# A planner that lays out one core's instructions: which tasks GpSimd may take, and when a tile may be taken early

## The chip, the core and the metric

The kernel runs on one core of one Trainium2 chip. The metric is the device time of one execution in microseconds (us). The core's engines work side by side: TensorE (PE in the profile; PEld is its weight load), VectorE (DVE), ScalarE (ACT), GpSimd (POOL) and SyncE (SP, which issues the transfers). Each engine runs its own instructions strictly in the order in which the program lists them, and waits where an operand is not there yet.

## The reference

Three layers follow each other, all in float32 (the weights come as float64 bit patterns, and are rounded on the chip):

```python
# 1. retention, B=2, H=8 heads, S=768, D=64
state = gamma * state + k[t] v[t]^T;  y[t] = scale * q[t] @ state
x = y.transpose(0, 2, 1, 3).reshape(1536, 512)
# 2. softplus layer, d_ff = 2048
h = x @ w_in;  x = (maximum(h, 0) + log1p(exp(-abs(h)))) @ w_out
# 3. gated layer, d_ff = 1536
xn = x / sqrt(mean(x * x, -1) + 1e-6) * rms_g
g = xn @ w_gate
out = (g / (1 + exp(-g)) * (xn @ w_val)) @ w_out2
```

## The kernel before

**Tiling.** The 1536 tokens are three blocks of 512 columns. A projection is a set of matmuls of 128x512. Every operand is split into a high and a low part (`hi` is a rounding copy, `lo` the rest), and each product is three matmuls. Blocks 0 and 1 go through a seven-product scheme (the class `Seven`, a Strassen form), which needs sums of activations (T1 to T4, and B11, B21, B22) and of weights (`s`, split into `ws_s`). The third block, "lone", is multiplied plainly. Its four output banks stay occupied in PSUM all through layer 2, so of eight banks four are left to turn over.

**Stages.** Until about 72 us the retention layer runs, written by hand in `batch`, `turn`, `scores` and so on. Everything after that is put into a `Plan` as tasks: layer 2 to about 302 us, then a passage in which the mean square of each block is taken (`mean`: TensorE sums squares, VectorE runs twelve tiny instructions on 128x4, called `small` and `root_t`), spread over the columns by TensorE and ScalarE (`along`, the tile `root`), multiplied in (`scaled`, L1185), and made into the B and T parts; then from about 361 us six passes over the gated layer (pass 0 begins within the passage).

**Weights.** A 128x512 weight takes eight tasks: ScalarE reads its low and high words (tiles `c` and `a`), VectorE shifts and joins bits (`w`, L880 and L883), GpSimd adds the integers (`c`, L886, called the total here), VectorE multiplies (`a`, L888), ScalarE rounds to `hi`, and VectorE or GpSimd subtracts for `lo`. 63 weights go through the plan.

**What sets the order.** The planner runs while the program is built. It gives every task a due time (`late`), followed back from TensorE's list, and then, step by step, starts the task that can start first by its own costs, on the engine that can take it. Tasks made with `("V", "G")` can go to VectorE or GpSimd (`less`, `rounded`, `part_lo`, the weight sums); GpSimd takes one only if its due time is at least `spare` us after its start. TensorE may take any of the next six products. What comes out is a fixed list of instructions for each engine; on the chip nothing is chosen any more. A task that opens a tile takes it from a pool (`R4`: two-wide tiles, `R2`: one-wide tiles, `PB`: PSUM banks, `ST`: landing tiles of the weight transfers). In `R4` and `R2` it is held back while fewer tiles are free than tasks with an earlier due time will want:

```python
ahead = 0 if p.loose else sum(1 for w in p.wanted if w < t.late - 1e-9)
if len(p.free) < n + ahead:
    return None
```

Helpers record many operations, so one line stands for many: L932 is every matmul of the plan, L828 every two-operand operation on SBUF tiles (`two_in`), L832 every copy of ScalarE.

Of the kernel before, what the change touches and what calls it, by code (L numbers as in the profile page):

```python
# [23 lines left out]
PAIRS = 2  # L24
WINDOW = 6
SLACK = 5.0
SPARE = 3.0
TINY = 1.125 * 2.0 ** -15


# [6 lines left out]
class Buf:  # L37

    def __init__(self, pool, name, dt=F32, tile=None, tag=None, at=0.0):
        self.pool, self.name, self.dt, self.tile, self.tag, self.last = pool, name, dt, tile, tag, at  # L40
        self.left, self.marks, self.opener = 0, {}, None


class Pool:

    def __init__(self, make, tags, at=0.0):
        self.make, self.free, self.wanted = make, [(at, tag) for tag in tags], []


class Task:  # L50
# [6 lines left out]

class Plan:

    def __init__(self, window=6, slack=3.0, spare=3.0):  # L60
        self.tasks, self.window, self.slack, self.spare = [], window, slack, spare

    def add(self, engs, took, do, reads=(), writes=(), opens=(), soft=False, rest=None):
        t = Task(engs, took, do, soft, rest or (took[0] if type(took) is tuple else took))
# [36 lines left out]
    def run(self, free):  # L101
        tasks = self.tasks
        at = 0.0
        for t in tasks:
            if t.engs == "P":
                t.nominal = at
                at += t.took
        for t in reversed(tasks):
            late = t.nominal if t.engs == "P" else at
            for h, off in t.heirs:  # L110
                late = min(late, h.late + off - t.rest - 0.05)
            if t.engs != "P":
                for b in t.bufs:
                    if b.pool and b.pool.psum:
                        ends = [w.nominal + w.took for w, _ in t.needs if w.engs == "P"]
                        if ends:
                            late = min(late, max(ends) + self.slack)
            t.late = late
        for t in tasks:
            for b in t.opens:  # L120
                b.pool.wanted.append(t.late)
            t.open_needs = len({id(o) for o, _ in t.needs})
            t.ready = 0.0
        for p in {id(b.pool): b.pool for t in tasks for b in t.opens}.values():
            p.wanted.sort()
        line = [t for t in tasks if t.engs == "P"]
        able = {e: [] for e in "AVGS"}
        for t in tasks:
            if not t.open_needs and t.engs != "P":
                for e in t.engs:  # L130
                    able[e].append(t)
        busy = {"V": 0.0, "G": 0.0}
        done = 0

        def start(t, e):
            st = max(free[e], max([o.end + LAT.get(o.eng + e, 0.06) - off for o, off in t.needs], default=0.0))
            want = {}
            for b in t.opens:
                want.setdefault(id(b.pool), [b.pool, 0])[1] += 1
            for p, n in want.values():  # L140
                ahead = 0 if p.loose else sum(1 for w in p.wanted if w < t.late - 1e-9)
                if len(p.free) < n + ahead:
                    return None
                st = max(st, sorted(p.free)[n - 1][0])
            if e == "V" and t.soft:
                st = max(st, busy["G"])
            if e == "G":
                st = max(st, busy["V"], busy["G"] + 0.02)
                if t.engs != "G" and t.late < st + self.spare:
                    return None  # L150
            return st

        while done < len(tasks):
            best = None
            for e in "PAVGS":
                if e == "P":
                    some = [t for t in line[:self.window] if all(o.end is not None for o, _ in t.needs)]
                else:
                    some = able[e]
                cands = [(start(t, e), n, t) for n, t in enumerate(some)]  # L160
                cands = [c for c in cands if c[0] is not None]
                if not cands:
                    continue
                first = min(c[0] for c in cands)
                near = [c for c in cands if c[0] <= first + 0.05]
                if e == "P":
                    pick = min(near, key=lambda c: c[2].nominal)
                    if pick[2] is not line[0] and any(len(b.pool.free) < 3 for b in pick[2].opens):
                        lead = [c for c in cands if c[2] is line[0] or not c[2].opens]
                        if lead:  # L170
                            first = min(c[0] for c in lead)
                            pick = min([c for c in lead if c[0] <= first + 0.05], key=lambda c: c[2].nominal)
                else:
                    pick = min(near, key=lambda c: (c[2].late, c[1]))
                if best is None or pick[0] < best[0] - 1e-9:
                    best = pick[0], e, pick[2]
            st, e, t = best
            for b in t.opens:
                p = b.pool
                p.free.sort()  # L180
                n = next(i for i, f in enumerate(p.free))
                _, b.tag = p.free.pop(n)
                p.wanted.remove(t.late)
                b.tile = p.make(b.tag, b)
            t.do(e)
            t.eng, t.start = e, st
            took = t.took[t.engs.index(e)] if type(t.took) is tuple else t.took
            t.end = st + (t.rest if e == "P" else took)
            free[e] = st + took - FILL.get(e, 0.0)
            if e == "S":  # L190
                free[e] = st + 0.06
                t.end = self.land(st, took)
            if e == "G":
                busy["G"] = t.end
            if e == "V" and t.soft:
                busy["V"] = t.end
            if e == "P":
                line.remove(t)
            else:
                for x in t.engs:  # L200
                    able[x].remove(t)
            for b in t.bufs:
                b.left -= 1
                b.last = max(b.last, t.end)
                if not b.left and b.pool:
                    b.pool.free.append((b.last + 0.06, b.tag))
            seen = set()
            for h, _ in t.heirs:
                if id(h) in seen:
                    continue  # L210
                seen.add(id(h))
                h.open_needs -= 1
                if not h.open_needs and h.engs != "P":
                    for x in h.engs:
                        able[x].append(h)
            done += 1
# [9 lines left out]
def retention_softplus_swiglu(ctx: ExitStack, tc: tile.TileContext, q, k, v, w_in, w_out,  # L226
# [28 lines left out]
    def row(tag, name, dt=F32):  # L255
        return mem.tile([P, N], dt, tag=tag, name=name)
# [207 lines left out]
    x, tr, tp = {}, {}, {}  # L464
# [337 lines left out]
    def two_wide(tag, b):  # L802
# [4 lines left out]
    R2 = Pool(lambda tag, b: row(tag, b.name, b.dt), [f"s2_{n}" for n in range(10)] + ["c0", "c1", "a0", "a1", "a2", "w", "s0", "s1"]  # L807
              + ["t0", "t1", "t2", "st", "fd", "r", "ms"], 3.0)
    PB = Pool(lambda tag, b: ps.tile([P, N], F32, tag=tag, name=b.name), [])
    PB.free = [(0.6 * n, f"ps{i}") for n, i in enumerate(oldest)]  # L810
    ST = Pool(lambda tag, b: mem.tile([P, N, 2], U32, tag=tag, name=b.name), st_free, 0.0)
    for p in (R4, R2, PB, ST):
        p.psum, p.loose = p is PB, p is PB or p is ST
    plan = Plan(WINDOW, SLACK, SPARE)
    add = plan.add
    A_PS, A_SB, V_2, G_2 = 0.6, 0.63, 0.69, 1.3

    def mine(pool, name, tile, tag, at=1.0):
        return Buf(pool, name, None, tile, tag, at)
# [103 lines left out]
    G = {key: mine(R4, "g", g_t[key], g_at[key]) for key in g_t}  # L923
# [36 lines left out]
    def psum(name):  # L960
        return Buf(PB, name)
# [89 lines left out]
    class Seven:  # L1051

        def __init__(self, nm, p):
            self.nm, self.p = nm, p
            self.Q, self.R, self.W = psum("Q"), psum("R"), psum("W")
# [326 lines left out]
    p = NPR - 1  # L1382
# [47 lines left out]
```

## Time and profile before

| | |
|---|---|
| median of 3 runs | 611.44 us (609.17 to 611.69) |
| the profiled execution's own time | 611.97 us |
| its span on the core | 610.1 us |
| PE busy | 593.9 us, 97% |
| DVE busy | 504.5 us, 83% |
| ACT busy | 359.3 us, 59% |
| POOL busy | 263.8 us, 43% |

The span runs from the first to the last instruction; the execution's own time is 1.9 us longer. The share of busy time is a mean over stages, so the prediction reads stretches of the span. A window row gives for each engine the busy time, the number of instructions in brackets, and then TensorE's granted clock as a share of full speed.

### The profile page before, as it was taken

To read this page: it belongs to the slowest core of one execution; us is meant where nothing else is said; L and a number is where in the kernel's file an instruction comes from. 1 tells how busy PE (TensorE), PEld (TensorE's weight loads), DVE (VectorE), ACT (ScalarE), POOL (GpSimd) and SP (SyncE) were. 2 spreads that over 40 slices of the span, in tenths; PEclk is the share of its full clock that TensorE was granted. 3 is DMA by queue.
4 is the path that set the end of the run, shared out by engine and by line. 5 is a ranking of instruction groups with operands and counts; after the bars stand their busy time and mean duration, and the time that the engine had idled before them with its cause. 6 is when DMAs were issued, how large, how long until landed. Compare 5 with 4: busy or idle time off the path is not lost.

```text
span 610.1 us, 8653 instructions
## 1 busy us (share of the span) xinstructions
PE 593.9 (97%) x3196; PEld 491.0 (80%) x3196; DVE 504.5 (83%) x775; ACT 359.3 (59%) x635; POOL 263.8 (43%) x204
## 2 busy tenths in 40 slices
PE   9999999999999999999979979999999999999997
PEld 8888878888778888888868858888888888888886
DVE  5788798989999988767798989997989989886355
ACT  3456587778748874877556666554644754653220
POOL 3544245323745534102542664466477455454000
PEclk9999999999999999999998989999999999999999
DMA  9999131213213320402200041322222212300014
GB/s 203 232 225 211 35 109 65 70 37 102 69 70 107 101 69 1 138 1 69 70 0 2 0 173 36 94 79 79 94 70 69 73 67 69 104 1 2 0 53 155
DMA packets 65562, 48.84 MB, mean 80 GB/s; under 512 B 39792, under 2 KB 60528, under 8 KB 65520
## 3 DMA queue, kind: packets, MB, share of 16 engines
q1 hardware_dynamic: 64320, 47.90, 27.5%
q8 instruction: 25, 0.41, 0.3%
q10 hardware_dynamic: 1200, 0.39, 0.3%
q14 instruction: 17, 0.14, 0.1%
HBM read 45.14 MB, written 3.15 MB: 79 GB/s over the span
## 4 chain that ended last, share of the span: by engine, by line
PE 87%; DVE 10%; issue 1%; DMA 1%; ACT 1%; DVEq 0%; SPq 0%; ACTq 0%
PE l L932 35%; PE Q L932 15%; PE R L932 7%; PE h L932 6%; PE h_w_gate L932 4%; PE h_w_val L932 4%; PE W L932 3%; PE h L617 3%; PE y L579 2%; PE sc L527 2%; PE pt L508 2%; DVE x L1185 1%; PE u L546 1%; DMA st_w_val<-in_moe_w_val_dram 1%; DVE T L828 1%
## 5 line engine op out<-in xcount | busy, mean ns | idle before, releaser
L886 POOL TENSOR_TENSOR c<-w,c 128x512 uint32<-128x512 uint32 x63 | 96.4, 1537 | 144.5 <-DVE w L883 91.3
L932 PE MATMUL l<-g,ws_w_out 128*128 128x512 f32 x576 | 137.3, 390 | 3.0 <-DVE x L1006 2.2
L932 PEld LDWEIGHTS l<-g,ws_w_out 128*128 128x128 f32 x576 | 107.7, 188 | 26.4 <-DVE x L1006 2.9
L932 PE MATMUL l<-ws_w_out,g 128*128 128x512 f32 x432 | 109.7, 394 | 3.3 <-ACT ws_w_out L832 3.3
L932 PEld LDWEIGHTS l<-ws_w_out,g 128*128 128x128 f32 x432 | 81.9, 190 | 21.8 <-ACT ws_w_out L832 3.7
L832 ACT ACTIVATE g<-t 128x512 fp32r<-128x512 f32 x78 | 47.7, 627 | 49.9 <-DVE t L828 21.2
L888 DVE SCALAR_TENSOR_TENSOR a<-a,c 128x512 f32<-128x512 f32 x63 | 57.3, 927 | 3.0 <-POOL c L886 1.5
L932 PE MATMUL Q<-T,ws_s 128*128 128x512 f32 x216 | 54.7, 390 | 0.1
L932 PE MATMUL h<-x,ws_w_in 128*128 128x512 f32 x216 | 51.2, 390 | 0.0
L832 ACT ACTIVATE p<-Q 128x512 f32<-128x512 f32 x44 | 26.3, 597 | 40.8 <-PE Q L932 40.7
L828 DVE TENSOR_TENSOR g<-t,g 128x512 fp32r<-128x512 f32 x53 | 43.7, 831 | 5.9 <-ACT g L832 5.6
L932 PEld LDWEIGHTS Q<-T,ws_s 128*128 128x128 f32 x216 | 40.5, 188 | 8.9 <-DVE T L828 0.5
L932 PEld LDWEIGHTS h<-x,ws_w_in 128*128 128x128 f32 x216 | 40.5, 188 | 8.6 <-issue 0.2
L828 POOL TENSOR_TENSOR g<-t,g 128x512 fp32r<-128x512 f32 x25 | 35.9, 1440 | 24.0 <-ACT g L832 23.9
L1284 DVE TENSOR_TENSOR o<-l,o 128x512 f32<-128x512 f32 x39 | 26.8, 688 | 15.8 <-PE l L932 15.7
L932 PE MATMUL h_w_val<-x,ws_w_val 128*128 128x512 f32 x144 | 34.5, 390 | 0.0
L932 PE MATMUL h_w_gate<-x,ws_w_gate 128*128 128x512 f32 x144 | 34.5, 391 | 0.0
L828 POOL TENSOR_TENSOR ws_s<-s,ws_s 128x512 fp32r<-128x512 f32 x15 | 20.8, 1387 | 25.6 <-ACT ws_s L832 25.6
L932 PEld LDWEIGHTS h_w_gate<-x,ws_w_gate 128*128 128x128 f32 x144 | 26.9, 188 | 5.8 <-ACT ws_w_gate L832 0.3
L932 PEld LDWEIGHTS h_w_val<-x,ws_w_val 128*128 128x128 f32 x144 | 27.0, 188 | 5.6
L832 ACT ACTIVATE ws_s<-s 128x512 fp32r<-128x512 f32 x36 | 22.4, 625 | 14.7 <-DVE s L828 9.3
L932 PE MATMUL R<-T,ws_s 128*128 128x512 f32 x108 | 27.2, 389 | 0.0
(187 smaller groups left out, 1184.2 us busy)
## 6 DMA issues: line engine op xcount, KB each, us to landing
st_w_out<-in_moe_w_out_dram SPq DMA_DIRECT2D x28, 512.0 KB, 3.4
st_w_in<-in_moe_w_in_dram SPq DMA_DIRECT2D x16, 512.0 KB, 4.4
st_w_gate<-in_moe_w_gate_dram SPq DMA_DIRECT2D x12, 512.0 KB, 3.6
st_w_val<-in_moe_w_val_dram SPq DMA_DIRECT2D x12, 512.0 KB, 3.6
v<-in_v_dram SPq DMA_DIRECT2D x12, 256.0 KB, 4.8
q<-in_q_dram SPq DMA_DIRECT2D x23, 128.0 KB, 4.9
k<-in_k_dram SPq DMA_DIRECT2D x23, 128.0 KB, 4.2
out_dram<-o SPq DMA_DIRECT2D x11, 256.0 KB, 2.0
```

The lines of the kernel that those rows point to most:

```text
L508: nc.tensor.transpose(pt[:, j, :], pair(qkv[g][i], j), ident)
L527: nc.tensor.matmul(sc[e][:, j, :], lhsT=t[r, 1, j, :], rhs=t[r, 0, j, :], start=True, stop=True)
L546: nc.tensor.matmul(u[e * D:(e + 1) * D, j, :], lhsT=kk[:, h, :], rhs=vv[:, NP * e + j, :], start=True, stop=True, skip_group_check=True)
L579: nc.tensor.matmul(ys[e][h * D:(h + 1) * D, i, n * P:(n + 1) * P], lhsT=lhsT, rhs=rhs, start=(e, h) not in begun, stop=last, skip_group_ch ...
L617: nc.tensor.matmul(h, lhsT=w[:, i, kk * P:(kk + 1) * P], rhs=src[j][kk // 2][:, kk % 2, :], start=(n == 0), stop=(n == 3 * KC - 1))
L828: {"V": nc.vector, "G": nc.gpsimd}[eng].tensor_tensor(out=out, in0=in0, in1=in1, op=op)
L832: nc.scalar.activation(out=out, in_=src, func=AF.Copy)
L886: add("G", G_2, lambda e: nc.gpsimd.tensor_tensor(out=c.tile, in0=w.tile, in1=c.tile, op=ALU.add), reads=[w, c], writes=[c])
L888: add("V", V_2, lambda e: nc.vector.scalar_tensor_tensor(out=a.tile, in0=a.tile, scalar=TINY, in1=c.tile.bitcast(F32), op0=ALU.is_ge, op1= ...
L932: nc.tensor.matmul(bank.tile, lhsT=lhsT(), rhs=rhs(), start=starts and k == 0, stop=stops and k == n - 1, skip_group_check=True)
L1185: add("V", 0.745, lambda e, a=a, m=m: nc.vector.scalar_tensor_tensor(out=a.tile, in0=a.tile, scalar=rg[:, m:m + 1], in1=root[b].tile, op0= ...
L1284: add("V", V_2, lambda e: nc.vector.tensor_tensor(out=o[2](), in0=bank.tile, in1=o[2](), op=ALU.add), reads=[bank, o[:2]], writes=[o[:2]])
```

## The change

GpSimd's threshold goes from 3 to 60 us, so that of the tasks which two engines can run it takes only those due 60 us later or more. A task that the rule on tiles would hold back may now start if the tiles that later tasks will hold, by their due times, leave `SPARED` = 4 free through the next 15 us for one-wide tiles, or up to 600 us for two-wide ones. Where the next tasks of VectorE and GpSimd would start within 0.1 us of each other, the one that asked first goes first.

```diff
-SPARE = 3.0
+SPARE = 60.0
+SPARED = 4
+HORIZON = 15
...
-        for p in {id(b.pool): b.pool for t in tasks for b in t.opens}.values():
+        pools = {id(b.pool): b.pool for t in tasks for b in t.bufs if b.pool}.values()
+        for p in pools:
             p.wanted.sort()
+            p.held = [0] * (int(at) + 40)
+        ends = {}
+        for t in tasks:
+            for b in t.bufs:
+                ends[b] = max(ends.get(b, 0.0), t.late + t.rest)
+        for b, end in ends.items():
+            if b.pool:
+                b.pool.size += not b.opener
+                for n in range(max(0, int(b.opener.late)) if b.opener else 0, int(end) + 1):
+                    b.pool.held[n] += 1
...
                 if len(p.free) < n + ahead:
-                    return None
+                    now = max(0, int(st - drift[0]))
+                    if len(p.free) < n or t.late < now + 2 or max(p.held[now:min(int(t.late), now + p.ahead)]) + n + self.spared > p.size:
+                        return None
                 st = max(st, sorted(p.free)[n - 1][0])
+            asked[t, e] = st
...
+                if e == "G" or e == "V" and pick[2].soft:
+                    lock[e] = pick
...
+            if e in lock and len(lock) == 2 and abs(lock["V"][0] - lock["G"][0]) < 0.1:
+                e = min("VG", key=lambda x: asked[lock[x][2], x])
+                st, _, t = lock[e]
...
-        p.psum, p.loose = p is PB, p is PB or p is ST
-    plan = Plan(WINDOW, SLACK, SPARE)
+        p.psum, p.loose, p.ahead = p is PB, p is PB or p is ST, HORIZON if p is R2 else 600
+    plan = Plan(WINDOW, SLACK, SPARE, SPARED)
```

The computation is the same; some instructions change their engine. GpSimd's plan shrinks from 168 instructions to the 63 totals, and VectorE's grows from 682 to 788: 105 come from GpSimd (74 are 512 elements wide, 31 are 256 wide), and one copy of 512 from ScalarE. The sequence of transfers does not change. Lines of the changed kernel are 28 higher from L828 on.

Three places show how the lists move. The first is GpSimd late in layer 3: before, sums (`s`), splits (`g`, `ws_s`, `ws_w_out`) and products (`t`) stand between the totals.

```order
L828 TENSOR_TENSOR t<-t,p_4026 128x512
L886 TENSOR_TENSOR c<-w,c 128x512
L828 TENSOR_TENSOR g<-t,g 128x512 x2
L828 TENSOR_TENSOR ws_s_4177<-s,ws_s_4177 128x512
L886 TENSOR_TENSOR c<-w,c 128x512 x2
L828 TENSOR_TENSOR s<-s,a 128x256
```

In the changed kernel one row stands for the whole plan on GpSimd, behind the last of the hand-written part:

```order
L422 TENSOR_TENSOR ws_w_out<-a,ws_w_out 128x512
L914 TENSOR_TENSOR c<-w,c 128x512 x63
```

All that stood between the totals has gone to VectorE.

The second place is VectorE just behind the first mean (block 0) at the start of the passage, between the last tiny instruction of the first root and the first two of the second (`ms_...` is the mean square of block 1). Before:

```order
L1169 SCALAR_TENSOR_TENSOR root_t_1069<-small_1070,root_t_1069 128x4
L1141 SCALAR_TENSOR_TENSOR x2_3194<-l2_1488,rg_97,x2_3189 128x512
L828 TENSOR_TENSOR sq_3171<-sq_3171,sq_3130 128x512
L828 TENSOR_TENSOR s_3197<-a_3137 128x256
L828 TENSOR_TENSOR sq_3171<-sq_3171,sq_3109 128x512
L828 TENSOR_TENSOR s_3197<-s_3197,a_2974 128x256
L1141 SCALAR_TENSOR_TENSOR x2_3194<-l2_1526,rg_97,x2_3189 128x512
L1185 SCALAR_TENSOR_TENSOR x2_1265<-x2_1265,rg_97,root_3219 128x512
L1185 SCALAR_TENSOR_TENSOR x2_1272<-x2_1272,rg_97,root_3219 128x512
L1185 SCALAR_TENSOR_TENSOR x2_1277<-x2_1277,rg_97,root_3219 128x512
L828 TENSOR_TENSOR B11_3237<-x2_1265,B11_3228 128x512
L1160 TENSOR_SCALAR small_1070<-ms_3232 128x4
```

And in the changed kernel:

```order
L1197 SCALAR_TENSOR_TENSOR root_t_1069<-small_1070,root_t_1069 128x4
L856 TENSOR_TENSOR sq_3242<-sq_3242,sq_3205 128x512
L916 SCALAR_TENSOR_TENSOR a_3082<-a_3082,c_3054 128x512
L856 TENSOR_TENSOR sq_3242<-sq_3242,sq_3184 128x512
L1169 SCALAR_TENSOR_TENSOR x2_3269<-l2_1484,rg_97,x2_3261 128x512
L911 SCALAR_TENSOR_TENSOR w_3207<-st_w_gate3_3108,w_3207 128x512
L856 TENSOR_TENSOR ws_w_gate_3267<-a_3082,ws_w_gate_3267 128x512
L1169 SCALAR_TENSOR_TENSOR x2_3269<-l2_1521,rg_97,x2_3261 128x512
L1188 TENSOR_SCALAR small_1070<-ms_3279 128x4
```

The three multiplications by the first root and the first B part now stand behind the second root, and weight work of pass 1 (`w_gate3`) stands among these rows. On TensorE the second `ms` has also gone ahead by one product: two products of twelve matmuls now stand between it and the second `root`, where one stood.

The third place is VectorE's split of the first two output weights of layer 3 (`w_out20`, `w_out21`), which the first products of the last layer read. Before, it stands at the end of the passage, behind the T4 part and among the splits of the activations `g`:

```order
L828 TENSOR_TENSOR T4_3535<-x2_1294,T4_3478 128x512
L880 TENSOR_SCALAR w_3547<-st_w_out21_3083 128x512
L883 SCALAR_TENSOR_TENSOR w_3538<-st_w_out20_2977,w_3538 128x512
L883 SCALAR_TENSOR_TENSOR w_3547<-st_w_out21_3083,w_3547 128x512
...
L888 SCALAR_TENSOR_TENSOR a_3372<-a_3372,c_3367 128x512
L888 SCALAR_TENSOR_TENSOR a_3397<-a_3397,c_3370 128x512
L828 TENSOR_TENSOR g_3524<-t_3390,g_3524 128x512
L828 TENSOR_TENSOR ws_w_out2_3590<-a_3372,ws_w_out2_3590 128x512
L828 TENSOR_TENSOR g_3567<-t_3463,g_3567 128x512
L828 TENSOR_TENSOR ws_w_out2_3593<-a_3397,ws_w_out2_3593 128x512
```

In the changed kernel it stands ahead of the whole passage, before the first tiny instruction:

```order
L916 SCALAR_TENSOR_TENSOR a_2897<-a_2897,c_2878 128x512
L916 SCALAR_TENSOR_TENSOR a_3051<-a_3051,c_2953 128x512
L1034 TENSOR_TENSOR x2_1373<-l2_3141,x2_1373 128x512
L856 TENSOR_TENSOR ws_w_out2_3178<-a_2897,ws_w_out2_3178 128x512
L856 TENSOR_TENSOR ws_w_out2_3181<-a_3051,ws_w_out2_3181 128x512
...
L1034 TENSOR_TENSOR x2_1443<-l2_3188,x2_1443 128x512
L1188 TENSOR_SCALAR small_1070<-ms_3212 128x4
```

Their last row stood 95 rows behind the first tiny instruction of the passage, and stands 7 rows ahead of it now.

## Rows read from the trace of the kernel before

**Rows 1.** Windows: us, busy time and instructions of each engine, granted clock, DMA share.

```profile
104.00:155.00 51.00, 51.00 (x226) 42.23 (x225) 46.29 (x76) 41.06 (x76) 16.93 (x12) 1.00 0.21 65
155.00:170.00 15.00, 12.77 (x56) 10.24 (x55) 14.44 (x19) 11.26 (x21) 8.70 (x6) 1.00 0.16 60
302.00:356.40 54.40, 47.70 (x218) 38.43 (x216) 49.73 (x95) 33.89 (x58) 26.61 (x18) 0.97 0.09 30
361.40:610.00 248.60, 245.20 (x1081) 202.46 (x1080) 197.86 (x288) 117.18 (x201) 114.86 (x88) 1.00 0.21 70
sum 537.60, PE 524.48 PEld 430.88 DVE 452.87 ACT 321.85 POOL 233.75; mean PE 74.93 PEld 61.55 DVE 64.70 ACT 45.98 POOL 33.39
```

**Rows 2.** Waits of PE after 72 us: total us, times, longest.

```profile
PE root L1178 <- DVE root_t L1169: 3.4, 1, 3.4
PE l L932 <- ACT ws_w_out L832: 3.3, 1, 3.3
PE l L932 <- DVE x L1006: 2.2, 1, 2.2
PE l L932 <- DVE ws_w_out L828: 0.7, 1, 0.7
```

**Rows 3.** Windows over the two stretches at a lower clock.

```profile
320.50:323.90 3.40, 3.40 (x10) 2.67 (x9) 3.32 (x6) 1.23 (x2) 0.00 (x0) 0.50 0.00 0
358.00:361.40 3.40, 3.39 (x8) 2.46 (x8) 3.40 (x8) 0.69 (x1) 1.74 (x1) 0.50 0.12 33
```

**Rows 4.** Chain of waits, 148 to 170 us: start, us, what.

```profile
149.97 5.45 PE l L932 x24
...
157.35 3.41 DVE t L956 x2
...
162.20 1.70 DVE g L828
...
167.79 0.69 DVE x L1006
```

**Rows 5.** Chain of waits through the passage, 296 to 362 us.

```profile
302.26 0.80 PE ms L1155 x8
...
305.84 0.17 DVE small L1168
...
309.58 0.34 DVE s L828
...
310.58 3.01 DVE x L1185 x3
313.58 1.70 DVE B L828
...
318.88 0.65 PE root L1178 x4
...
333.68 0.66 DVE x L1185
...
336.21 1.81 DVE x L828 x3
...
348.17 0.34 DVE w L880
...
350.71 4.46 DMA st_w_val<-in_moe_w_val_dram
...
356.43 1.92 PE l L932 x5
```

**Rows 6.** Groups by line and form: busy us, mean ns of one, idle time before.

```profile
L886 POOL TENSOR_TENSOR c<-w,c 128x512 uint32<-128x512 uint32 x63 | 96.4, 1537 | 144.5 <-DVE w L883 91.3 <-ACT c L876 34.8 <-ACT a L878 9.9
L888 DVE SCALAR_TENSOR_TENSOR a<-a,c 128x512 f32<-128x512 f32 x63 | 57.3, 927 | 3.0 <-POOL c L886 1.5 <-ACT a L878 1.3
L828 POOL TENSOR_TENSOR g<-t,g 128x512 fp32r<-128x512 f32 x25 | 35.9, 1440 | 24.0 <-ACT g L832 23.9
L1284 DVE TENSOR_TENSOR o<-l,o 128x512 f32<-128x512 f32 x39 | 26.8, 688 | 15.8 <-PE l L932 15.7
```

More of the change, by code (lines that the diff above doesn't have):

```diff
@@ L47, in __init__ @@
         self.make, self.free, self.wanted = make, [(at, tag) for tag in tags], []
+        self.size = len(tags)
 class Task:
@@ L58, with __init__ @@
 class Plan:
-    def __init__(self, window=6, slack=3.0, spare=3.0):
-        self.tasks, self.window, self.slack, self.spare = [], window, slack, spare
+    def __init__(self, window=6, slack=3.0, spare=3.0, spared=2):
+        self.tasks, self.window, self.slack, self.spare, self.spared = [], window, slack, spare, spared
     def add(self, engs, took, do, reads=(), writes=(), opens=(), soft=False, rest=None):
@@ L131, in run @@
                     able[e].append(t)
-        busy = {"V": 0.0, "G": 0.0}
+        drift = [0.0]
+        busy, asked = {"V": 0.0, "G": 0.0}, {}
         done = 0
@@ L153, in run @@
         while done < len(tasks):
-            best = None
+            best, lock = None, {}
             for e in "PAVGS":
@@ L183, in run @@
                 p.wanted.remove(t.late)
+                for n in range(max(0, int(st - drift[0])), max(0, int(t.late))):
+                    p.held[n] += 1
                 b.tile = p.make(b.tag, b)
@@ L197, in run @@
             if e == "P":
+                drift[0] = max(drift[0], st - t.nominal)
                 line.remove(t)
@@ L206, in run @@
                     b.pool.free.append((b.last + 0.06, b.tag))
+                    for n in range(max(0, int(t.end - drift[0])) + 1, int(ends[b]) + 1):
+                        b.pool.held[n] -= 1
             seen = set()
```

## The prediction

> **What bounds the kernel now.** I read the windows first, to see where TensorE is not full. From 104 to 155 us it is busy throughout, and from 361.4 to 610 it misses only the last 3.4 us, where the outputs drain; between them it loses 2.2 us in the window from 155 to 170 and 6.7 in the one from 302 to 356 [rows 1]. Where it is full it cannot go faster: 24 matmuls take 5.45 us [rows 4], 0.227 each, and the plan has 2,268 of that form on either side of the change. So the change can only give back waits, or add some.
>
> The waits of TensorE after 72 us are four: 3.4 us for the second root, 3.3 for a weight of the last layer, 2.2 for a bank of PSUM that VectorE's add (L1006) sets free, and 0.7 for a weight near 84 us, together 9.6 [rows 2]. The two long ones cost more than themselves. Behind each stands a stretch of 3.4 us in which TensorE was granted half its clock, 1.2 GHz instead of 2.4 [rows 3]. At half speed 3.4 us do the work of 1.7, so the two cost another 3.4. In all **13.0 us** can be had: 10.1 in the passage between the layers (3.4 + 3.3 + 3.4), 2.2 at 166 us, 0.7 at 84.
>
> Who is late at these places? The chain of waits runs through VectorE both times. It is VectorE that is held up by GpSimd: two instructions L956 take 3.41 us and one split 1.70 [rows 4], three multiplications L1185 take 3.01 where one elsewhere takes 0.66, and one B part 1.70 [rows 5]. The groups show the same: L888, whose two inputs lie in SBUF, has a mean of 927 ns; L1284, which reads one input from PSUM, has 688 [rows 6].
>
> **What the move costs VectorE.** Its unhindered pitch is 0.60 us for 512 elements (three in 1.81), 0.34 for 256 and for the shift L880, 0.66 for L1185 and its like, 0.19 for a tiny one (0.17 and 0.02 of issue) [rows 5]. The plan before has 508, 43 + 63, 32 and 36 of them: 304.8 + 36.0 + 21.1 + 6.8 = 368.8 us. It was busy for 452.9 [rows 1]. The 84 between are mostly time held by GpSimd's 168 instructions, 0.50 each.
>
> The change adds 75 x 0.60 + 31 x 0.34 = 55.5 us of work to VectorE and takes 105 of the 168 blockers away, 52.5 at that mean. Load: 424.3 + 63 x 0.50 = 455.8, against 452.9. **Over the plan the move is free for VectorE; it comes out as shorter hand-overs.** What I don't know is the price of a remaining total: nothing if VectorE happens to read PSUM, as L1284's 688 ns show; at most 1.28 if it stands for the whole of one (96.4 us over 63 is 1.53 with GpSimd's own waits, and a split's 1.70 less 0.60 leaves 1.10 of standing [rows 4, 6]). I take the mean of 0.50, because it comes from the same instructions, and keep 0 and 1.28 for the range.
>
> One rule speaks against the move. The row: VectorE is already busy for 46.3 of the 51 us from 104, and for 14.4 of the 15 from 155 [rows 1]. The Trainium skill (Perfetto Trace Analysis, Optimizing Scalar/DVE Operations) says that work may be offloaded from a saturated VectorE, even to GpSimd; this change does the reverse. It adds that the two share a read port, so that shifting work between them might not help. By the first half alone VectorE's busy time would be 452.9 + 55.5 = 508.4; by the row's blocked time it is 455.8. That first half is the slower rival below.
>
> **The passage (10.1 us to be had).** Three things move, and the lists show them.
>
> - The second `ms` goes one product earlier on TensorE, so that 24 matmuls (5.4 us) instead of 12 (2.7) cover the twelve tiny instructions. VectorE no longer has three L1185 and a B part ahead of them (3.01 + 1.70 [rows 5]).
> - `w_out20` and `w_out21` are finished before the passage, so the 3.3 us wait for them has nothing left to wait for. The DMA of 4.46 us in that chain [rows 5] fetched a later weight and stood there only because ScalarE read it before it rounded `w_out2`.
> - GpSimd has one total to run in the passage, where it was busy for 26.6 us [rows 1].
>
> Is VectorE then fast enough? I count its rows from the first tiny instruction (303.1 us) to the split of the second `g` that the first output product reads: 42 x 0.60 + 12 x 0.66 + 36 x 0.19 = 40.0 us, which ends at 343.1, or 344.4 with one full block. TensorE's product began at 356.4 [rows 5]; freed of 3.4, 3.3 and 1.7 us it comes at 348.0. On the way, the first product on T1 stands behind three `ms` of 0.80 us, three `root` of 0.65 and 108 matmuls of 0.227, so T1 is due at 302.3 + 2.4 + 1.95 + 24.5 = 331.1; VectorE has done it after 25.6 us, at 328.7. T3 is due 24 matmuls later, at 336.5, and done after 31.0 us, at 334.1. So it suffices, with 2.4 us in hand at the tightest place. Some of that goes in waits of VectorE on ScalarE's roundings, which the sum leaves out. I take 1.1 us of stall as left, too short for the clock to fall (it fell only after waits of 3.3 and 3.4). **-9.0 us.**
>
> **The early weight (0.7).** Near 84 us VectorE's split of the first weight stands three rows earlier, and a sum for a T part and a split of `g` that stood ahead of it come later. **-0.7.**
>
> **The dense stretch (the wait at 166 us).** Here VectorE gets more to do. Between the copies of block 0's last output of group 0 and the add of its counterpart (324 matmuls, 73.4 us of TensorE, about 104 to 180 us) it had 80 x 0.60 + 22 x 0.34 = 55.5 us; now it has 98 x 0.60 + 25 x 0.34 = 67.3, and 10 totals at 0.50 make 72.3. That is 1.1 below TensorE's time, so the stretch is as full as it was. Between the adds around the old wait there were about 10 us of rows; now there are about 12, less held up. I leave the 2.2 us wait standing and **add 1.0**. Between free totals (67.3, the wait may vanish) and dear ones (67.3 + 12.8 = 80.1, 6.7 more of waiting) this is the largest unknown.
>
> **The last layer (no wait now).** Its heaviest pass has 204 matmuls, 46.2 us; VectorE now has 54 x 0.60 + 18 x 0.34 + 4 x 0.66 = 41.2 us in it, 44.7 with 7 totals. This had no wait to lose, and the margin shrinks, from about 9 us to 1.5. **+1.0** for a hand-over or two that come late.
>
> Sum: -9.0 - 0.7 + 1.0 + 1.0 = -7.7. The profiled execution took 611.97 us, 0.5 above the median of the runs, so its sum stands for the median too within what three runs tell: 612.0 - 7.7 = **604.3 us**. GpSimd becoming late itself costs nothing: it needs about 63 x 1.5 = 95 us in 530, and its totals were waiting on VectorE, not the reverse (91.3 us of idle time for `w` [rows 6]).
>
> **The rivals.**
>
> 1. *The waits of the passage only move* (chance 0.13). VectorE's chain from root to T parts is long, and if hand-overs to ScalarE eat the margin of 2.4 us and some 7 more, TensorE stands before T1 or T3 instead, long enough for the clock to fall. For it: the margin is small against 40 us of rows. Against it: 4.9 us are in hand at the end of the chain. Time: 612.0 - 0.7 + 1 + 1 less some 3, about 610.
> 2. *Half of it* (0.20). One wait of some 3 us stays in the passage, with a clock dip of 1.7 behind it: 604.3 + 3.6 = 607.9, or less. This still counts as faster.
> 3. *VectorE becomes the bound* (0.09, slower). A total costs its full 1.28 us, since nearly all of VectorE's new work has both inputs in SBUF. Then the dense stretch asks for 6.7 us more than TensorE's time, and the two heaviest passes for 39.4 + 8 x 1.28 - 46.2 = 3.4 and 41.2 + 7 x 1.28 - 46.2 = 4.0: 612.0 - 9.7 + 14.1 = 616.4. It decides from a price of about 1.1 us for each total, where the three together (4.9 + 2.0 + 2.7) use up the gain of 9.7. For it: VectorE's windows of 91 and 96% [rows 1]; against it: 0.50 is what such instructions cost so far. The saturation rule of the skill's page above would end here.
>
> **How the numbers follow.** My forecast has 0.58, the rivals 0.20, 0.13 and 0.09. If all waits went and no new one came, 612.0 - 13.0 = 599.0: the low end. The high end takes in rival 2 and most of rival 1: 609.5. Outside lie rival 3 and a part of rival 1, under 2 in 10. A measurement of this kernel can tell about 0.5%, 3.1 us; so faster is below 608.3: 0.58 + most of 0.20, 0.77; the same: 0.13; slower: 0.10.
>
> **What would show it.** Right: GpSimd with 63 instructions in the plan; L888 near 800 ns and no three L1185 in 3 us; no wait of TensorE for a root or `ws_w_out` over 1.5 us in the passage, and the clock at 1.00 through it. VectorE's busy time should stand within 10 us of the old 504.5 plus 3. Wrong: a wait of more than 3 us before a Q or R product on a T part, or PSUM waits on L1034 that add up to over 6 us before 245 us, or waits in the last passes on VectorE's splits.

## The result, and the profile after

The changed kernel took 596.22 us (median of 4 executions, 595.56 to 596.97), the kernel before 611.57 (4 executions, 609.17 to 613.88). The ratio is 0.975, with a 95% interval of 0.971 to 0.979: faster by 15.35 us, twice the 7.7 that was forecast, and below the range of 599.0 to 609.5. The profiled execution took 596.97 us, with a span of 595.2.

The windows of the changed kernel over the stretches of [rows 1], with the sum over the plan (columns as there: us, then busy time and instructions of PE, PEld, DVE, ACT and POOL, granted clock, DMA share, GB/s):

```profile
104.00:155.00 51.00, 51.00 (x227) 42.23 (x226) 48.09 (x83) 42.79 (x78) 13.42 (x8) 1.00 0.26 81
155.00:170.00 15.00, 15.00 (x68) 12.43 (x67) 14.95 (x28) 11.94 (x22) 2.98 (x2) 1.00 0.22 78
...
302.00:356.40 54.40, 53.69 (x251) 44.46 (x250) 51.02 (x101) 35.59 (x61) 4.28 (x3) 1.00 0.09 30
...
sum 522.60, PE 518.20 PEld 428.70 DVE 450.12 ACT 319.71 POOL 93.79; mean PE 86.37 PEld 71.45 DVE 75.02 ACT 53.29 POOL 15.63
```

TensorE is full from 104 to 170 us, where it lost 2.2 us before, although VectorE is now busy for 48.09 + 14.95 of those 66 us where it had 46.29 + 14.44. In the passage TensorE lacks 0.7 us, and the clock stays at 1.00. Over the plan VectorE is busy for 450.1 us with 790 instructions, where it had 452.9 with 685.

TensorE's waits in the plan, the whole list (total us, times, longest):

```profile
PE Q L960 <- DVE B L856: 0.7, 1, 0.7
```

This one line stands where [rows 2] had four. The groups that answer to [rows 6]:

```profile
L914 POOL TENSOR_TENSOR c<-w,c 128x512 uint32<-128x512 uint32 x63 | 93.8, 1494 | 382.3 <-DVE w L911 252.4 <-ACT t L1229 24.3 <-ACT t L981 24.1
L916 DVE SCALAR_TENSOR_TENSOR a<-a,c 128x512 f32<-128x512 f32 x63 | 44.1, 707 | 5.7 <-POOL c L914 5.6
L1312 DVE TENSOR_TENSOR o<-l,o 128x512 f32<-128x512 f32 x39 | 26.8, 688 | 16.3 <-PE l L960 16.3
```

The product `a` fell from 927 to 707 ns, close to L1312, which reads PSUM. The chain of waits through the passage (start, us, what), against [rows 5]:

```profile
297.93 3.52 DMA st_w_val<-in_moe_w_val_dram
...
308.92 1.99 DVE x L1213 x3
310.91 0.60 DVE B L856
...
312.83 2.34 PE Q L960 x9
```

Three multiplications take 1.99 us where they took 3.01, the B part 0.60 where it took 1.70, and no transfer stands in front of an output product any more.

For the account I add up what TensorE's matmuls of the plan take from start to start beyond their pitch of 0.227 us, where that is over 0.1 us. This counts what the list of waits leaves out: the slow restart behind a wait (0.11 us each) and the half-clock stretches. It is 15.28 us before and 1.22 after, a difference of 14.06. Small excesses fell by 0.36. The plan began 0.87 us earlier (71.53 for 72.40) behind code that is unchanged; over the 20 profiles of this study that start lies between 71.0 and 76.0, so I take this for chance.

### The profile page after: what moved, and what is told of

Its sections match the earlier page's. It is cut to its first block, busy times and chain, and to the rows that moved or that the text cites. A ratio compares the mean times of both kernels' runs of the same rounds, so it can differ in the third digit from the quotient of the medians.

```text
span 595.2 us, 8619 instructions
## 1 busy us (share of the span) xinstructions
PE 588.4 (99%) x3196; PEld 489.8 (82%) x3196; DVE 502.5 (84%) x881; ACT 358.0 (60%) x634; POOL 123.8 (21%) x99
## 4 chain that ended last, share of the span: by engine, by line
PE 86%; DVE 7%; ACT 4%; DMA 1%; issue 0%; DVEq 0%
PE l L960 31%; PE Q L960 15%; PE R L960 8%; PE h L960 6%; PE h_w_gate L960 6%; PE h_w_val L960 5%; PE W L960 4%; PE y L607 3%; PE h L645 3%; PE sc L555 2%; PE pt L536 2%; DMA st_w_val<-in_moe_w_val_dram 1%; DVE t L984 1%; PE u L574 1%; DVE g L856 1%; DVE x L1034 1%
## 5 line engine op out<-in xcount | busy, mean ns | idle before, releaser
L914 POOL TENSOR_TENSOR c<-w,c 128x512 uint32<-128x512 uint32 x63 | 93.8, 1494 | 382.3 <-DVE w L911 252.4
L960 PE MATMUL l<-ws_w_out,g 128*128 128x512 f32 x432 | 108.0, 389 | 0.0
L856 DVE TENSOR_TENSOR g<-t,g 128x512 fp32r<-128x512 f32 x78 | 52.9, 689 | 2.6 <-ACT g L860 2.6
L916 DVE SCALAR_TENSOR_TENSOR a<-a,c 128x512 f32<-128x512 f32 x63 | 44.1, 707 | 5.7 <-POOL c L914 5.6
L1312 DVE TENSOR_TENSOR o<-l,o 128x512 f32<-128x512 f32 x39 | 26.8, 688 | 16.3 <-PE l L960 16.3
L856 DVE TENSOR_TENSOR ws_s<-s,ws_s 128x512 fp32r<-128x512 f32 x36 | 25.4, 706 | 1.4 <-ACT ws_s L860 1.4
L982 ACT ACTIVATE t<-t 128x512 f32<-128x512 f32 x42 | 26.3, 628 | 0.4
```

The lines of the kernel that those rows point to most:

```text
L856: {"V": nc.vector, "G": nc.gpsimd}[eng].tensor_tensor(out=out, in0=in0, in1=in1, op=op)
L914: add("G", G_2, lambda e: nc.gpsimd.tensor_tensor(out=c.tile, in0=w.tile, in1=c.tile, op=ALU.add), reads=[w, c], writes=[c])
L916: add("V", V_2, lambda e: nc.vector.scalar_tensor_tensor(out=a.tile, in0=a.tile, scalar=TINY, in1=c.tile.bitcast(F32), op0=ALU.is_ge, op1= ...
L960: nc.tensor.matmul(bank.tile, lhsT=lhsT(), rhs=rhs(), start=starts and k == 0, stop=stops and k == n - 1, skip_group_check=True)
L982: add("A", A_SB, lambda e: nc.scalar.activation(out=t.tile, in_=t.tile, func=AF.Exp, scale=-1.0), reads=[t], writes=[t])
L1312: add("V", V_2, lambda e: nc.vector.tensor_tensor(out=o[2](), in0=bank.tile, in1=o[2](), op=ALU.add), reads=[bank, o[:2]], writes=[o[:2]])
```

## The experiments

Three theories. **A, the engine:** VectorE, held up less by GpSimd, hands over sooner, wherever the plan puts the work; this is the prediction's own ("it comes out as shorter hand-overs"). **B, the early tiles:** weights and the second mean square are placed ahead of the passage because tiles are taken early. **C, the order:** what counts is the sequence that the three rules give together, whoever executes it.

**The three rules apart.** The edits on the changed kernel, singly or in pairs, are these: the old spare number; no early tile; no turns.

```diff
-SPARE = 60.0
+SPARE = 3.0
...
-                    now = max(0, int(st - drift[0]))
-                    if len(p.free) < n or t.late < now + 2 or max(p.held[now:min(int(t.late), now + p.ahead)]) + n + self.spared > p.size:
-                        return None
+                    return None
...
-            if e in lock and len(lock) == 2 and abs(lock["V"][0] - lock["G"][0]) < 0.1:
+            if False and e in lock and len(lock) == 2 and abs(lock["V"][0] - lock["G"][0]) < 0.1:
```

Spare number alone: 

> Only the spare number (60) is kept: GpSimd does the totals alone, no tile is taken early, no turns. Theory A (the gain comes from VectorE being held up less by GpSimd, wherever the plan puts the work): nearly the whole gain, 596 to 600 us, and no wait of TensorE over 1.5 us in the passage, no half-clock stretch. Theory B (the gain comes from weights and the second ms being placed earlier because tiles are taken early): the wait for a weight of the last layer comes back with a half-clock stretch behind it, 3.3 + 1.7 us or both waits of the passage, 10.1 us: 601 to 607 us. If VectorE's busy time in the plan stays near 450 us, the price of a GpSimd instruction is the 0.4 us worked out from the changed kernel.

Early tiles alone: 

> Only the early opening of tiles is kept: the spare number is 3 again, so GpSimd gets its splits, multiplications and parts back, and no turns are modelled. Theory A: the hand-overs of VectorE are as long as before (products with both inputs in SBUF near 900 ns, some rows of 1.7 to 3.4 us), so most of the 9.6 us of waits are still there in some place: 606 to 612 us. Theory B: the long waits of the passage are gone although GpSimd is as busy as before (some 200 us): 597 to 602 us.

Turns alone: 

> Only the rule that VectorE and GpSimd take turns when they would start together is kept; spare number 3, no early opening. Both theories: about the time before, 609 to 613 us, with waits of TensorE that add up to about 9 us, though in other places perhaps. If it gains more than 3 us, the order that the rule gives at ties matters, and neither theory is enough.

Spare number and early tiles: 

> The spare number and the early opening without the turns. Both theories: within 2 us of the changed kernel, 595 to 598 us, no wait of TensorE over 1.5 us in the plan. If it is 3 us or more slower, the turns carry a part of the gain in their own right, together with one of the other two parts.

Spare number and turns: 

> The spare number and the turns, without the early opening of tiles. The run with the spare number alone took 608.4 us and still had the wait for the last layer's weight with its half-clock stretch (5.9 us together) and 3.2 us of waits for T parts ahead of it. Theory B (the passage's weight wait is a matter of early opening alone): it stays here, 603 to 609 us. If the turns by themselves can place the weight in time: 598 to 602 us.

Early tiles and turns: 

> The early opening and the turns, with the spare number 3, so that GpSimd keeps its splits, multiplications and parts. The run with early opening alone took 608.8 us with some 4.2 us lost in the dense stretch near 166 us. Theory A (a held-up VectorE makes the dense stretch late): 3 to 5 us stay there, 603 to 609 us. Theory C (the turns give the order that matters, whoever does the work): no wait over 1.5 us there, 597 to 601 us.

| rules kept | us | ratio to before, 95% interval |
|---|---|---|
| spare number | 608.39 | 0.995 (0.993 to 0.997) |
| early tiles | 608.81 | 0.994 (0.991 to 0.997) |
| turns | 617.75 | 1.009 (1.006 to 1.013) |
| spare number, early tiles | 602.05 | 0.983 (0.979 to 0.987) |
| spare number, turns | 604.46 | 0.989 (0.983 to 0.994) |
| early tiles, turns | 618.14 | 1.009 (1.006 to 1.013) |
| all three | 596.22 | 0.975 (0.971 to 0.979) |

Neither A nor B as stated: the spare number alone gives 3.5 us, early tiles alone 3.1, where each theory wanted most of 15. The spare number alone came above both ranges, but left the wait for the last layer's weight standing (3.4 us), as B said; early tiles alone came in A's range. The spare number with the turns came in B's range, yet not as B had it: the wait for that weight fell to 0.7 us without any early tile. The other three missed every range, so the turns play a part that neither theory gave them: they cost where the spare number is 3 (5.8 us alone, 9.3 with early tiles) and gain where it is 60 (3.9 without early tiles, 5.8 with them). Each row is one order, and small planner numbers move the time by up to 11.7 us (last table of this section), so no rule's share is shown by one row. Where the turns cost, it is in a new place: with turns alone TensorE lost 10.8 us between 83 and 107. The chain of waits of that run there:

```profile
89.04 3.74 DMA st_w_in<-in_moe_w_in_dram
...
92.80 0.67 ACT c L902
93.47 0.55 ACT a L904
94.03 0.52 ACT g L858
94.55 0.53 ACT ws_w_out L858
```

ScalarE reads a later weight (`st_w_in`), whose transfer has only begun, before it rounds the one that TensorE needs. It is the pattern that the kernel before has in the passage [rows 5], moved to another place by another order.

**Order and engine apart.** Two kernels swap them. The first keeps the changed order and gives GpSimd back the 105 instructions that it had (74 of 512 elements and 31 of 256; the text on record says 75), each at its new place. The second keeps the order before, and VectorE executes those 105.

```diff
-            t.do(e)
+            t.do("G" if tasks.index(t) in GIVEN else e)
```

```diff
-            t.do(e)
+            t.do("V" if e == "G" and "V" in t.engs else e)
```

> The changed kernel's order on every engine, with the 105 instructions that GpSimd had before (75 of 128x512, 31 rows that are half as wide among its splits and sums) given back to GpSimd, each at its place in the new order. Theory C (the order gives the gain, not the engine): by the run with 26 splits given back, which took 1.75 us more than the changed kernel, some 3 to 6 us more for 105: 598 to 603 us. Theory A (freeing VectorE of GpSimd's instructions gives the gain): most of it is lost, 606 to 614 us.

> The kernel before with its order on every engine, and the same 105 instructions run on VectorE at their places. Theory A: the waits shrink with the blocked time, 600 to 606 us. Theory C: the same places stay late, since the order has them late: the weight of the last layer (3.3 us and its half-clock stretch) and the second root: 608 to 613 us.

Measured: new order on the old engines 605.91 us (ratio 0.989, 0.986 to 0.992), old order on the new engines 608.09 (0.992, 0.989 to 0.995). Order alone gives 6.0 us, engine alone 3.8 (the two intervals overlap), both together 15.4. The first time lies between the ranges of C and A, the second above A's and at the low end of C's: each theory was half right. The profile of the old order is of its slowest execution, 611.52 us, in which TensorE stood 3.0 us ahead of the plan; counted from the plan's start, order alone takes away some 5 us of excess and engine alone some 4. The excess of TensorE's matmuls by place (us) shows what each takes away:

| place | before | old order, VectorE | new order, GpSimd | changed |
|---|---|---|---|---|
| 84 us, weight | 1.0 | 0.2 | 0 | 0 |
| 104 to 200 us | 2.5 | 0 | 1.7 | 0 |
| 272 us | 0 | 0 | 2.0 | 0.1 |
| 305 to 325 us, second root or B parts | 5.3 | 3.9 | 6.1 | 1.0 |
| 325 to 350 us, T parts | 0.3 | 0.8 | 0.7 | 0 |
| 352 to 362 us, weight of the last layer | 5.8 | 6.0 | 0 | 0 |

The weight of the last layer goes with the order alone. TensorE's waits in the passage, old order with VectorE doing the work:

```profile
PE l L932 <- ACT ws_w_out L832: 4.0, 1, 4.0
PE Q L932 <- DVE B L828: 1.4, 1, 1.4
PE root L1178 <- DVE root_t L1169: 0.3, 1, 0.3
```

and the chain of waits in front of the first line:

```profile
350.03 4.93 DMA st_w_val<-in_moe_w_val_dram
354.99 0.66 ACT c L876
355.65 0.53 ACT ws_w_out L832
```

ScalarE stands at the later weight's transfer, and freeing VectorE does nothing for it. The new order with GpSimd at work has no such line:

```profile
PE Q L966 <- ACT B L866: 1.3, 2, 0.7
PE ms L1189 <- DVE sq L862: 0.8, 1, 0.8
PE Q L966 <- DVE B L862: 0.7, 1, 0.7
...
PE root L1212 <- DVE root_t L1203: 0.3, 1, 0.3
```

Here the second mean and the B parts are late instead. VectorE's chain at the second root is held up too: one tiny instruction takes 1.27 us, as the chain of waits shows, while GpSimd executes an addition of the squares.

```profile
313.45 1.27 DVE small L1201
314.72 0.02 issue
314.74 0.17 DVE small L1202
```

So the wait for the second root falls from 3.4 to 0.3 us by either part alone, but either alone leaves the B parts behind it late, by 1.4 us (old order) or 2.0 (new), with a half-clock stretch behind them. Only both together leave 0.7 us and the clock at 1.00. Here, and at 272 us, the parts give more together than apart.

The dense stretch goes with the engine. The new order alone shortens the wait near 166 us as well, to 0.4, but leaves 1.7 us in all between 125 and 197. The same rows of VectorE, from the pair of products to the add for which TensorE waited [rows 4], in windows of the kernel before and then of the old order on VectorE:

```profile
156.06:167.79 11.73, 10.23 (x46) 8.13 (x44) 11.73 (x16) 8.25 (x16) 7.93 (x5) 1.00 0.10 42
```

```profile
158.81:166.84 8.03, 8.03 (x37) 6.63 (x36) 8.03 (x17) 7.95 (x16) 0.00 (x0) 1.00 0.15 59
```

Before, 14 rows (the two others counted are neighbours at the edges) take 11.73 us, of which 8 at 0.60 and 6 at 0.34 are 6.8 of unhindered work: five splits of GpSimd in a block hold VectorE for 4.9 us, 0.98 each. With two rows more (two of the five splits; the other three stand outside the window) and no GpSimd, VectorE takes 8.03 us, which is its unhindered pitch (10 x 0.60 + 6 x 0.34 = 8.04). The timeline of VectorE before shows where the time goes:

```profile
157.26 3.50 DVE L956 SCALAR_TENSOR_TENSOR t<-p,t 128x512 f32<-128x512 f32 x2
160.68 0.68 DVE L1006 TENSOR_TENSOR x<-l,x 128x512 f32<-128x512 f32 x1
```

The two L956 read SBUF twice and take 1.75 us each; the add L1006 between them and the next splits reads PSUM and takes 0.68, with a split of GpSimd running beside it. This agrees with the Trainium skill (GPSIMD Engine Reference, Specifications), which says that GpSimd's way to SBUF is shared with VectorE and is contended for by VectorE instructions with two inputs in SBUF.

**Some of the splits back, as a dose.** In the changed kernel every third split of `g` goes to GpSimd, 26 of 78.

```diff
-        add(("V", "G"), (V_2, G_2), lambda e: two_in(e, buf.tile[:, 1], src.tile, buf.tile[:, 0].bitcast(F32), ALU.subtract),
+        to_g = buf.name == "g" and turn_g[0] % 3 == 0
+        add(("V", "G"), (V_2, G_2), lambda e: two_in("G" if to_g else e, buf.tile[:, 1], src.tile, buf.tile[:, 0].bitcast(F32), ALU.subtract),
```

> The order of the changed kernel on every engine but one thing: every third split of g (26 of the 78 on VectorE) is given to GpSimd, at the place that it has in the order. Theory C (the order is what counts, not the engine): within 2 us of the changed kernel, 595 to 599 us. Theory A (GpSimd's instructions cost more in hand-overs than they take off VectorE): a split takes 1.43 us on GpSimd where VectorE takes 0.69, so each that TensorE waits for comes 0.75 us or more later, behind a total up to 2.2 us: waits of TensorE on g come up, 600 to 610 us.

Measured: 597.97 us (0.977, 0.972 to 0.982), within C's bounds and not to be told from the changed kernel. The windows over the plan, of this kernel and then of the one with all 105 given back:

```profile
72.40:595.00 522.60, 518.25 (x2302) 428.69 (x2300) 450.48 (x764) 319.81 (x565) 134.18 (x89) 1.00 0.21 67
```

```profile
72.40:604.50 532.10, 523.01 (x2302) 429.06 (x2300) 451.61 (x685) 319.91 (x565) 232.98 (x168) 1.00 0.20 66
```

VectorE is as busy with 764 or 685 instructions as with 790: 450.5, 451.6 and 450.1 us. What it no longer executes it stands for, 0.61 us for each of the 26 (15.6 us of work and 0.4 more busy time) and 0.54 for each of the 105 (54.9 and 1.5). In this order, giving work to GpSimd relieves VectorE of nothing. In the old order it does in part. With the 105 on VectorE there, the window over the plan is this:

```profile
76.01:609.50 533.49, 523.85 (x2306) 430.80 (x2304) 466.43 (x790) 322.11 (x567) 95.82 (x63) 0.99 0.20 66
```

VectorE is busy for 466.4 us, and for 452.9 with them on GpSimd [rows 1], 13.6 less. So moving the work alone made VectorE busier, and the new order of the same instructions took 16.3 us off: what a GpSimd instruction costs VectorE depends on the rows that stand beside it.

**More work on VectorE.** One more instruction behind each product `a`:

```diff
+            nc.vector.tensor_tensor(out=c.tile, in0=c.tile, in1=c.tile, op=ALU.bitwise_or)
```

> The changed kernel with 63 more VectorE instructions that the planner does not know of, each of 128x512 behind an L916 product: some 0.6 us each, 38 us in all, VectorE's busy time in the plan 450 to 488 of 518 us. The step that failed in the prediction took VectorE as all but full from 104 to 170 us. If it is full there in the sense that TensorE waits for each instruction added, the 10 or so that fall there cost 6 us, and those of the other dense passes more: 606 us or above. If its busy rows hide slack (rows that began early and wait for their input inside), under 3 us: 596 to 600 us.

Measured: 620.45 us (1.014, 1.009 to 1.019), 24.2 more than the changed kernel; between 104 and 180 us TensorE's excess rose from 0 to 6.6 us. So VectorE has no slack there, as the prediction read it; a stretch with VectorE this full can still be free of waits, if the order puts the right row first.

**The rules or one good draw?** Four small changes of the planner's numbers were tried on both sides: `SLACK` 6.0, `SLACK` 4.0 (for 5.0), a GpSimd instruction planned at 1.7 us (for 1.3), a VectorE instruction at 0.75 (for 0.69). With the planner of the change GpSimd keeps its 63 totals in each (with the changed slack, one instruction more).

```diff
-SLACK = 5.0
+SLACK = 6.0
```

```diff
-    A_PS, A_SB, V_2, G_2 = 0.6, 0.63, 0.69, 1.3
+    A_PS, A_SB, V_2, G_2 = 0.6, 0.63, 0.75, 1.3
```

The changed kernel, slack 6.0: 

> The changed kernel with one number of the planner changed, SLACK 6.0 for 5.0: the order moves, GpSimd keeps but the totals (and one or two more). Theory A: the engines' load is the same, 595 to 598 us. Theory C: another order, and a time that may lie several us off, 596 to 606 us.

The changed kernel, VectorE at 0.75: 

> The changed kernel with another number of the planner changed: a VectorE instruction of 128x512 is planned at 0.75 us for 0.69. GpSimd has the same 63 totals. Theory A: 595 to 598 us. Theory C: another order, 596 to 606 us.

The kernel before, slack 6.0: 

> The kernel before with SLACK 6.0 for 5.0 in its planner. If the gain belongs to the rules (theory R): within some 4 us of before, 608 to 616 us, above the changed kernel with the same number (595.2). If the gain is a draw of the order (theory D): anywhere from 596 to 618 us.

The kernel before, VectorE at 0.75: 

> The kernel before with a VectorE instruction of 128x512 planned at 0.75 us. Theory R: 608 to 618 us, above the changed kernel with the same number (606.9). Theory D: 596 to 618 us, as often below it as above.

The kernel before, GpSimd at 1.7: 

> The kernel before with a GpSimd instruction of 128x512 planned at 1.7 us for 1.3. Theory R: 606 to 616 us. Theory D: 596 to 618 us.

The changed kernel, GpSimd at 1.7: 

> The changed kernel with a GpSimd instruction of 128x512 planned at 1.7 us for 1.3; GpSimd has the same 63 totals. Theory R: 595 to 607 us, at least 5 us under the kernel before with the same number. Theory D: 596 to 618 us.

The kernel before, slack 4.0: 

> The kernel before with SLACK 4.0 for 5.0 in its planner. Theory R (the gain belongs to the rules): 606 to 618 us. Theory D (the gain is a draw of the order): 596 to 618 us.

The changed kernel, slack 4.0: 

> The changed kernel with SLACK 4.0 for 5.0. Theory R: 595 to 607 us, at least 5 us under the kernel before with the same number. Theory D: 596 to 618 us.

| number | planner before, us (ratio, interval) | planner of the change, us (ratio, interval) |
|---|---|---|
| as it was | 611.57 | 596.22 (0.975, 0.971 to 0.979) |
| slack 6.0 | 617.29 (1.011, 1.004 to 1.018) | 595.23 (0.972, 0.971 to 0.974) |
| slack 4.0 | 617.28 (1.007, 1.004 to 1.010) | 597.79 (0.976, 0.973 to 0.979) |
| GpSimd at 1.7 | 615.65 (1.009, 1.004 to 1.013) | 604.59 (0.990, 0.985 to 0.994) |
| VectorE at 0.75 | 616.39 (1.007, 1.000 to 1.014) | 606.89 (0.992, 0.989 to 0.994) |

The six kernels priced by theory R (the gain belongs to the rules) and D (one good draw) came in R's range but for slack 6.0 on the kernel before, 1.3 us above it. Of the two that were still priced by A and C, 595.23 lies in A's range and 606.89 above both.

The gain belongs to the rules: the five pairs differ by 9.5 to 22.1 us, 15.5 in the mean, and the slowest median of the one side lies 4.7 us below the fastest of the other. But within one side a number that says nothing of the work moves the time by up to 11.7 us. All five of the planner before lose at least 5 us between 305 and 325 us and at least 5 between 350 and 363; of the five of the change, three lose no more than 1.0 in the whole passage, and the two slow ones lose 7 to 8 between 340 and 360. With slack 6.0 TensorE has no wait in the plan at all, and its executions (594.94 to 595.36) all lie below those of the changed kernel, though the two were not timed side by side: it is the fastest version found, by some 1 us.

## Why the prediction failed on the size

By its own steps, in the matmuls' excess:

| step | forecast | measured |
|---|---|---|
| passage | -9.0 | -10.4 (11.4 lost before, 1.0 left) |
| early weight | -0.7 | -1.0 |
| dense stretch | +1.0 | -2.5 |
| last layer | +1.0 | -0.1 |
| sum | -7.7 | -14.1 (from unrounded terms) |

- **The step that failed is the dense stretch.** "I leave the 2.2 us wait standing and add 1.0" rested on the load of 73 us, with each GpSimd instruction at the mean of 0.50 us. The wait hung on 12 us, in which five GpSimd splits in a block cost 0.98 each. The run with the old order on VectorE shows that without them the same rows take 8.03 us for 11.73, and the wait is gone. A mean over the plan says nothing on a place where the blockers stand together. This is 3.5 of the 6.4 us by which the sum was short.
- **"In all 13.0 us can be had" was too small**, and with it the low end of the range. The list of waits and the half-clock windows leave out 0.11 us for each restart, 0.34 at 339 us, and gaps of which the largest is 0.4, at 357.8: start to start it is 15.3. So the passage gave 1.4 more than its forecast, though the stall left in it was sized well (1.1 forecast, 1.0 measured).
- **The last layer's +1.0** was a charge for a margin that shrank. A margin of 1.5 us that stays positive costs nothing; TensorE is full there.
- The move being free for VectorE was right in the total, 455.8 forecast and 450.1 measured, but partly by luck. A total has no one price: 0.41 us in the new order (450.1 less 424.3 of work, over 63), 0.67 in the old one (466.4), for the 0.50 forecast. The move alone cost VectorE 13.6 us, and the order gave 16.3 back.
- What did not hold is the sentence behind it, that the gain comes out as shorter hand-overs: by itself that is 3.8 us of 15.4. The passage's three moves were named rightly, and that the weight came in time was the doing of the order, as the prediction had it. But "the chain of waits runs through VectorE both times" was wrong for that weight: with VectorE freed in the old order TensorE still waited 4.0 us, behind ScalarE's read of a later weight.
- Rival 3 priced a total at 1.28 us and needed about 1.1. The measured 0.41, and 0.67 in the old order, rule it out. The Trainium skill (Perfetto Trace Analysis, Optimizing Scalar/DVE Operations) says that work may be offloaded from a saturated VectorE, even to GpSimd, and that between these two engines it might not help. The new order agrees with the second half (450.1, 450.5 and 451.6 us for 63, 89 and 168 GpSimd instructions); in the old order a quarter of the work came off (466.4 us for 63, 452.9 for 168).
- Rivals 1 and 2 did not come here, but the same rules with two other numbers give such cases: 604.6 and 606.9 us, with 7 to 8 us lost late in the passage.

Open: why the turns gain only beside the spare number of 60. Which tie of the planner puts ScalarE's read of a later weight ahead of the rounding that is due was not traced.

## What to carry to other kernels

Price a blocker where it stands, from the unhindered pitch of the very rows in front of the wait, not by a mean over the program. Measure what is to be had from start to start of the bound engine's instructions; the waits that a list names were 9.6 of 15.3 us here. Where a planner sets the order, separate order from engine by executing one order on the other's engines, and try its numbers a little to each side before believing a size: the sign held in five pairs, the size lay between 9.5 and 22.1 us.

## What had not been expected of the hardware

TensorE's clock does not fall by the length of a wait alone. The kernel before waits 2.2 us at 166 us and keeps its clock; the windows across and behind that wait (columns as above):

```profile
165.50:169.00 3.50, 1.27 (x6) 0.77 (x5) 3.50 (x9) 3.50 (x7) 0.00 (x0) 1.00 0.00 0
169.00:172.40 3.40, 3.40 (x17) 2.77 (x16) 3.16 (x6) 2.58 (x5) 0.66 (x1) 1.00 0.00 0
```

The old order on VectorE was granted half, 1.2 GHz, behind waits of 0.3 and 1.4 us in the passage, where TensorE had been busier (1.65 of 3.40 us for 1.27 of 3.50):

```profile
315.60:319.00 3.40, 1.65 (x8) 1.17 (x9) 3.37 (x8) 1.66 (x3) 0.00 (x0) 1.00 0.00 0
319.00:322.40 3.40, 3.40 (x9) 2.63 (x9) 3.40 (x7) 1.23 (x2) 0.00 (x0) 0.50 0.00 0
```

The prediction's remark that the clock fell only after waits of 3.3 and 3.4 us held for one trace. What decides it is not settled by these runs.
